# First and last transform stage on four 64x64 quarters of the PE array, third stage in two halves through one PSUM bank

## The chip, the core and the metric

The kernel runs on one core of a Trainium2 chip. A core has a matrix engine (TensorE; PE in the profile, its weight loads PEld), VectorE (DVE), ScalarE (ACT), GpSimd (POOL) and SyncE (SP), whose queue issues all DMAs of this kernel. Data lies in SBUF and PSUM, both with 128 partitions; matmuls write PSUM, which has 8 banks of 2 KB per partition. A matmul holds one operand as weights in the array and streams the other through it. The metric is the device time of one execution in microseconds (us).

## The reference

A Fourier layer on 8 sequences of 3136 x 256 float32 values, then a gated feed-forward layer with a convolution of three taps:

```python
X = np.fft.rfft(x, axis=1)
Yr = Xr @ w_r - Xi @ w_i + b_r
Yi = Xr @ w_i + Xi @ w_r + b_i
Yr = np.sign(Yr) * np.maximum(np.abs(Yr) - lam, 0.0)      # and Yi
y = np.fft.irfft(Yr + 1j * Yi, n=3136, axis=1)
h = np.maximum(y @ w_in, 0.0)                             # 256 -> 1024
conv_out[t] = sum(conv_w[k] * h[t + k - 1] for k in range(3))
out = (h * sigmoid(conv_out)) @ w_out                     # 1024 -> 256
```

## The kernel before

The transform of 3136 = 49 x 64 points is done by tables, in four stages.

Stage 1 takes transforms of 49 points. A row n of x is read as (n, j) with 98 values of n and 32 of j; x rows of even and odd n belong to two different transforms, so that a table `f1` of 98 x 98 holds two 49-point transforms beside each other, with zeros between. The work of one sequence (batch, 8 of them) is cut into 8 chunks of 4 values of j. A chunk is loaded by `load_x` into `xr` (98 partitions x 4 x 256), `stage1` makes two float32 matmuls of 512 columns, ScalarE copies each into `a1`, and one DMA stores `a1` in DRAM (`sc1`). `stage1_head` does the 8 chunks of the first batch at the start, all at once.

Stage 2 (`load_a2`, `stage2`) takes 64-point transforms of groups of 4 frequencies; `mix` multiplies by the complex weights in split precision (36 matmuls, `ps_mx`, L329), `threshold` cuts, and `stage3` transforms back by 64 points (12 matmuls, L361, into a PSUM tile of two banks, one copy of 1024 columns, one store to `sc2`). 50 groups (items) go through this as a software pipeline: iteration `it` does stage 2 of item `it`, the mix of item `it - 1`, the threshold of `it - 2` and stage 3 of `it - 3`. The order of PE, DVE and ACT is the order in which the code is written here. Stage 1 of the later batches is put between, as pieces that `one(k)` gives out at four places of an iteration; the numbers `due` say how many pieces are to be done by when (13 pieces in five iterations in the steady part, two pieces to a chunk).

In the second part, `stage4` takes the last transform, back by 49 points. It loads `z2` from `sc2` (100 partitions, 4 values of j, 256 values); z2 is the weights and the table `i2` (100 x 98, two 49-point transforms with zeros between) is streamed, in 8 matmuls per call; ScalarE and VectorE split the result into `yh` and `yl`. Then `up` and `down` do the feed-forward layer in chunks of 448 rows: 12 matmuls of 450 columns (L528), VectorE and ScalarE work for taps and gate, 21 matmuls of 256 columns (L556). The 8 calls of `stage4` per batch are put between these, for the batch after the one that the feed-forward layer is in; a scheduler at build time sets the final order of this part. All work of the first part must be done before its memory is free for the second.

float32 matmuls (stages 1, 2 and 4) show in the trace as two records each; those of type F32R show as one.

Of the kernel before, what the change touches and what calls it, by code (L numbers as in the profile page):

```python
# [9 lines left out]
F32 = mybir.dt.float32  # L10
# [9 lines left out]
R = 49  # L20
R2 = 64
# [14 lines left out]
def _tables():  # L36
    n = np.arange(R)
    n2 = np.arange(R2)
    u = np.arange(U + 1)

    f = np.zeros((R, 2, U + 1))
    ang = 2 * np.pi * ((n[:, None] * u[None, :]) % R) / R
    f[:, 0, :] = np.cos(ang)
    f[:, 1, :] = -np.sin(ang)
    fwd1 = np.zeros((R, 2, 2 * R))
    for h in range(2):
        for uu in range(1, U + 1):
            for c in range(2):
                fwd1[:, h, (uu - 1) * 4 + c * 2 + h] = f[:, c, uu]
# [6 lines left out]
    inv2 = np.zeros((2, 2 * (U + 1), R, 2))  # L56
    for i in range(2):
        inv2[i, :, :, i] = g.reshape(2 * (U + 1), R)
# [34 lines left out]
    return {  # L93
        "fwd1": fwd1.reshape(2 * R, 2 * R).astype(np.float32),
        "fwd2": fwd2.reshape(2 * R2, (U + 1) * 2 * SP).astype(np.float32),
        "inv1": inv1.reshape(2 * SP, U + 2, 2, 2, H).transpose(0, 1, 4, 3, 2).reshape(2 * SP, (U + 2) * 2 * R2).astype(np.float32),
        "inv2": inv2.reshape(4 * (U + 1), 2 * R).astype(np.float32),
    }


# [1 line left out]
def spectral_ffn_kernel(ctx: ExitStack, tc: tile.TileContext, x, w_r, w_i, b_r, b_i,  # L102
                        w_in, conv_w, w_out, fwd1, fwd2, inv1, inv2, out):
    nc = tc.nc
    K1, K2, KQ, KI = 2 * R, 2 * SP, 2 * R2, 4 * (U + 1)
# [16 lines left out]
    with ExitStack() as ab:  # L122
# [12 lines left out]
        f1 = c1.tile([K1, P], F32, name="f1")[:, 0:K1]  # L135
        t2 = c1.tile([KQ, U + 1, K2], F32, name="t2")
        cmx.tile([P, 96], F32, name="pad")
        bias = cmx.tile([P, 2, D], F32, name="bias")
# [101 lines left out]
                    yield None  # L240
                yield from work

        def load_x(pool, b, jc, parts=1, **kw):

            xr = pool.tile([K1, JC, D], F32, name="xr", **kw)
            xv = x[b].rearrange("(n j) d -> n j d", j=H)[:, jc * JC:(jc + 1) * JC, :]
            w = JC // parts
            for k in range(0, JC, w):
                ld = nc.sync.dma_start(xr[:, k:k + w, :], xv[:, k:k + w, :])
            return xr, ld  # L250

        def stage1(b, jc, xr):

            a1 = s1p.tile([K1, JC, D], F32, name="a1", bufs=3)
            for j in range(0, JC, 2):
                ps = ps1.tile([K1, 2, D], F32, name="ps_s1")
                nc.tensor.matmul(ps, f1, xr[:, j:j + 2, :], start=True, stop=True)  # L257
                nc.scalar.copy(a1[:, j:j + 2, :], ps)
                if j + 2 == JC:
                    nc.sync.dma_start(sc1[b][:, jc * JC:(jc + 1) * JC, :], a1)  # L260
                yield None

        def stage1_head(xs, b=0):

            with tc.tile_pool(name="ha", bufs=1, reuse_waits="tile") as ha:
                for jc, xr in enumerate(xs):
                    a1 = ha.tile([K1, JC, D], F32, name=f"ha{jc}")
                    for j in range(0, JC, 2):
                        k = (jc * 2 + j // 2) % 4
                        if k < 3:  # L270
                            ps = psm.tile([K1, 2, D], F32, name="ps_s1h", tag=f"ps_mx{k}")
                        else:
                            ps = ps1.tile([K1, 2, D], F32, name="ps_s1")
                        nc.tensor.matmul(ps, f1, xr[:, j:j + 2, :], start=True, stop=True)
                        if j:
                            nc.vector.tensor_copy(a1[:, j:j + 2, :], ps)
                        else:
                            nc.scalar.copy(a1[:, j:j + 2, :], ps)
                    st = nc.sync.dma_start(sc1[b][:, jc * JC:(jc + 1) * JC, :], a1)
            return st  # L280

        def load_a2(b, g):
# [71 lines left out]
        def stage3(b, g, s):  # L354

            sh, sl = s
            ps = psa.tile([KQ, UG, D], F32, name="ps_s3")
            for k in range(UG):
                u = g * UG + k if g < NG else U + k % 2
                for n, (lt, rh) in enumerate(((i1_hi, sh), (i1_hi, sl), (i1_lo, sh))):  # L360
                    nc.tensor.matmul(ps[:, k, :], lt[:, u, :], rh[:, k, :], start=(n == 0), stop=(n == 2))  # L361
            z1 = io.tile([KQ, UG, D], F32, name="z1", bufs=2)
            nc.scalar.copy(z1, ps)
            if g < NG:
                nc.sync.dma_start(sc2[b][:, g * UG:(g + 1) * UG, :], z1)
            else:
                for k in range(UG):
                    nc.sync.dma_start(sc2[b + k][:, U, :], z1[:, k, :])

        def some(g, n):  # L370
            for _ in range(n):
# [56 lines left out]
        for it in range(n_it + 3):  # L428
            xs[it], vs[it - 1] = [], []
            two = stage2(items[it][1], a2s.pop(it), xs[it]) if it < n_it else iter(())  # L430
            mx = mix(xs.pop(it - 1), vs[it - 1]) if 0 <= it - 1 < n_it else iter(())
            due = (2, 5, 9, 13, 16)[it] if it < 5 else 16 + 3 * (it - 4) if it <= 10 else 34 + 13 * (it - 10) // 5
            n_a, given = due - given, due
            work = 5 <= it < n_it

            def one(k=0):
# [17 lines left out]
            some(mx, 8)  # L454
            back(1)
            ss[it - 2] = next(th, None)
            one(1)
            some(two, 1)
            some(mx, 5)
            if it - 1 in i1s:  # L460
# [2 lines left out]
            some(th, 1)  # L463
            some(two, 1)
            back(1)
            some(mx, 5 if n_a > 3 else 9)
            one(2)
            some(th, 1)
            some(mx, 9)
            one(3)  # L470
            some(mx, 64)
            if held:
                held[:] = [0] * (next(background, None) == "act")
            if 0 <= it - 3 < n_it:
                stage3(*items[it - 3], ss.pop(it - 3))
            one(0)
            if it + 2 < n_it:
                a2s[it + 2], ld = load_a2(*items[it + 2])

# [8 lines left out]
    wk.tile([P, 24], F32, name="pad", bufs=1)  # L488
    psh, pso = pool("psh", 2, space=PSUM), pool("pso", space=PSUM)

    JG = 4
    NPC = H // JG

    def new_y(b):
        y = [(y_a, y_b)[b % 2].tile([P, NT, SW], F32R, name=nm) for nm in ("yh", "yl")]
# [3 lines left out]
            nc.vector.memset(qf[:, :, S + 1:S + 2], 0.0)  # L499
        return y  # L500

    def stage4(b, jg, y):

        z2 = zio.tile([KI, JG, D], F32, name="z2")
        nc.sync.dma_start(z2, sc2[b].rearrange("(j q) u e -> (q u) j e", q=4)[:, jg * JG:(jg + 1) * JG, :])
        ps = psh.tile([P, NT, 512], F32, name="ps_s4", tag="ps_h")
        for t in range(NT):
            for j in range(JG):
                nc.tensor.matmul(ps[:, t, j * K1:(j + 1) * K1], z2[:, j, t * P:(t + 1) * P], i2, start=(j == 0), stop=(j == JG - 1),  # L509
                                 skip_group_check=True)  # L510
        src = ps[:, :, 0:JG * K1].rearrange("p t (j m) -> p t m j", j=JG)

        def view(q):
            return q[:, :, 1:S + 1].rearrange("p t (m j) -> p t m j", j=H)[:, :, :, jg * JG:(jg + 1) * JG]
        nc.scalar.copy(view(y[0]), src)
        nc.vector.tensor_tensor(view(y[1]), src, view(y[0].bitcast(F32)), op=ALU.subtract)  # L516

# [109 lines left out]
```

## Time and profile before

| | us |
|---|---|
| median of 3 runs | 1760.06 (1758.44 to 1760.09) |
| the profiled execution, its own time | 1759.99 |
| span of its trace | 1758.2 |
| chain of work that ended last: share of stage 1 (L257) | 5% |
| the same: stage 4 (L509) | 6% |
| the same: feed-forward (L528, L556) | 31% and 31% |
| the same: mix (L329), stage 2 (L301), stage 3 (L361) | 11%, 5%, 3% |

The span runs from the first to the last instruction; the rest of the time lies around it. A row of a group gives line, engine, operation, tiles, shapes and count, then the busy time in us and the mean time of one in ns, then the idle time of the engine before them and what ended it. Records of matmuls overlap, since one is issued while the one before it still runs: the spacing of starts is what a matmul costs in a dense row, not its length. A row of the timeline or of the chain gives start, length, engine, line and how many like it stand together.

### The profile page before, as it was taken

The numbers are of one execution on the slowest core, as the hardware profiler recorded it, in microseconds if no ns is written. First come the engines' busy times: TensorE is split into PE (matmuls) and PEld (weight loads), VectorE is DVE, ScalarE is ACT, GpSimd is POOL, SyncE is SP. The second block draws the span as 40 slices with busy tenths as digits, with TensorE's granted clock in tenths as the row PEclk, the third lists the DMA queues.
The fourth block names the chain that finished last, engine by engine and source line by source line (L and its number), as shares of the span: only waits on it lengthen the run. The fifth ranks groups of instructions, "written<-read, shape, count | busy, mean of one in ns | idle before, by whom it ended". The sixth has DMA issues, their size and how long they took to land.

```text
span 1758.2 us, 28865 instructions
## 1 busy us (share of the span) xinstructions
PE 1721.6 (98%) x11872; PEld 1602.2 (91%) x11872; DVE 1472.0 (84%) x1757; ACT 1206.8 (69%) x1565; POOL 118.7 (7%) x54
## 2 busy tenths in 40 slices
PE   5999999999999999999999999999999999999999
PEld 2788888888988999999999999999999999999998
DVE  2778988889995988888888888888888888888887
ACT  2567677677665777677777777777777777777766
POOL 0122222222230000000000000000000000000000
PEclk8999999999998999999999999999999999999999
DMA  7877777767434110111111011111101111100001
GB/s 223 256 233 240 226 230 237 232 204 234 141 104 126 42 48 22 41 50 50 41 50 50 22 40 50 50 40 50 50 22 41 50 50 41 50 22 22 22 22 43
DMA packets 108305, 165.48 MB, mean 94 GB/s; under 512 B 8492, under 2 KB 86316, under 8 KB 108174
## 3 DMA queue, kind: packets, MB, share of 16 engines
q1 hardware_dynamic: 108174, 163.64, 29.4%
q8 instruction: 94, 1.54, 0.4%
q14 instruction: 37, 0.30, 0.1%
HBM read 86.02 MB, written 77.59 MB: 93 GB/s over the span
## 4 chain that ended last, share of the span: by engine, by line
PE 93%; DMA 2%; DVE 2%; issue 1%; ACT 0%; SPq 0%; DVEq 0%; ACTq 0%
PE ps_h L528 31%; PE acc L556 31%; PE ps_mx L329 11%; PE ps_s L509 6%; PE ps_s L257 5%; PE ps_s L301 5%; PE ps_s L361 3%; DMA t<-in_fwd_dram 1%; DMA z<-sc 1%; DVE v L337 0%; DMA sc<-a 0%; DVE p L333 0%; DMA sc<-ha 0%; DVE fl L307 0%; DVE v L348 0%
## 5 line engine op out<-in xcount | busy, mean ns | idle before, releaser
L556 PE MATMUL acc<-wout,gh 128*128 128x256 f32 x3136 | 567.4, 280 | 0.0
L528 PE MATMUL ps_h<-yh,win 128*128 128x450 f32 x1792 | 550.6, 368 | 0.0
L537 DVE SCALAR_TENSOR_TENSOR c<-h,cw,c 128x896 f32<-128x896 f32 x448 | 512.9, 1147 | 38.9 <-ACT c L535 37.3
L556 PEld LDWEIGHTS acc<-wout,gh 128*128 128x128 f32 x3136 | 490.1, 188 | 5.1
L556 PE MATMUL acc<-wout,gl 128*128 128x256 f32 x1568 | 437.4, 280 | 0.0
L530 ACT ACTIVATE h<-ps_h 128x900 f32<-128x900 f32 x224 | 207.4, 926 | 261.1 <-PE ps_h L528 261.1
L528 PEld LDWEIGHTS ps_h<-yh,win 128*128 128x128 f32 x1792 | 339.4, 189 | 26.1 <-DVE yl L516 0.4
L528 PE MATMUL ps_h<-yl,win 128*128 128x450 f32 x896 | 329.7, 368 | 0.0
L543 DVE TENSOR_TENSOR gl<-c,gh 128x896 fp32r<-128x896 f32 x224 | 243.0, 1088 | 76.3 <-ACT gh L542 74.7
L556 PEld LDWEIGHTS acc<-wout,gl 128*128 128x128 f32 x1568 | 293.8, 188 | 0.6
L539 DVE TENSOR_TENSOR c<-h,c 128x896 f32<-128x896 f32 x224 | 243.1, 1086 | 48.2 <-ACT c L538 48.2
L542 ACT CAST gh<-c 128x896 fp32r<-128x896 f32 x224 | 211.0, 942 | 70.2 <-DVE c L539 68.3
L538 ACT ACTIVATE c<-c 128x896 f32<-128x896 f32 x224 | 213.0, 951 | 8.2 <-DVE c L537 4.4
L329 PE MATMUL ps_mx<-wmix_hi,fl 128*128 128x256 f32 x600 | 185.2, 309 | 2.8 <-DVE fl L311 2.8
L329 PE MATMUL ps_mx<-wmix_hi,fh 128*128 128x256 f32 x600 | 183.7, 306 | 0.7 <-DVE v L337 0.6
L528 PEld LDWEIGHTS ps_h<-yl,win 128*128 128x128 f32 x896 | 169.4, 189 | 11.0
L535 ACT ACTIVATE c<-h,cw 128x896 f32<-128x896 f32 x168 | 176.1, 1048 | 2.2 <-DVE gl L543 0.2
L329 PE MATMUL ps_mx<-wmix_lo,fh 128*128 128x256 f32 x600 | 168.6, 281 | 0.0
L351 POOL TENSOR_TENSOR sl<-v,sh 128x1024 fp32r<-128x1024 f32 x50 | 118.5, 2370 | 410.7 <-PE ps_s L361 254.1
L337 DVE TENSOR_TENSOR v<-ps_mx,p 64x512 f32<-64x512 f32 x200 | 137.4, 687 | 2.9
L301 PEld LDWEIGHTS ps_s<-t,a 128*128 128x128 f32 (+1 forms) x800 | 99.7, 198 | 39.6 <-issue 28.8
L509 PEld LDWEIGHTS ps_s<-i,z 100*128 100x128 f32 x1024 | 128.1, 198 | 5.8 <-issue 3.0
(84 smaller groups left out, 1959.2 us busy)
## 6 DMA issues: line engine op xcount, KB each, us to landing
z<-sc SPq DMA_DIRECT2D x64, 400.0 KB
xr<-in_x_dram SPq DMA_DIRECT2D x63, 392.0 KB
a<-sc SPq DMA_DIRECT2D x48, 512.0 KB
sc<-z SPq DMA_DIRECT2D x48, 512.0 KB
out_dram<-o SPq DMA_DIRECT2D x27, 896.0 KB
sc<-a SPq DMA_DIRECT2D x56, 392.0 KB
sc<-ha SPq DMA_DIRECT2D x8, 392.0 KB
win_bits<-in_moe_w_in_dram SPq DMA_DIRECT2D x4, 512.0 KB
```

The costliest lines, as they stand in the source:

```text
L301: nc.tensor.matmul(ps[:, k], a2[0:rows, k, t * P:(t + 1) * P], t2[0:rows, u, :], start=(k == 0), stop=(k == UG - 1), skip_group_check=True)
L329: nc.tensor.matmul(ps[c][:, k, :], lt, rh, start=(n == 0), stop=(n == len(mm) - 1))
L509: nc.tensor.matmul(ps[:, t, j * K1:(j + 1) * K1], z2[:, j, t * P:(t + 1) * P], i2, start=(j == 0), stop=(j == JG - 1), skip_group_check=True)
L528: nc.tensor.matmul(ps[:, a, 0:CH + 2], lt, rh, start=(n == 0), stop=(n == len(mm) - 1))
L530: nc.scalar.activation(h, ps[:, :, 0:CH + 2], AF.Relu)
L535: nc.scalar.mul(c, h[:, :, 0:CH], cw[:, 0, f:f + 1])
L537: nc.vector.scalar_tensor_tensor(c, h[:, :, k:k + CH], cw[:, k, f:f + 1], c, op0=ALU.mult, op1=ALU.add)
L538: nc.scalar.activation(c, c, AF.Sigmoid)
L539: nc.vector.tensor_tensor(c, h[:, :, 1:CH + 1], c, op=ALU.mult)
L542: nc.scalar.copy(gh, c)
L543: nc.vector.tensor_tensor(gl, c, gh.bitcast(F32), op=ALU.subtract)
L556: nc.tensor.matmul(acc[m // 2][:, m % 2, :], lt[:, sl], rh[:, f, :], start=(f == 0 and n == 0 and m % 2 == 0), stop=(f == NF - 1 and n == ...
```

## The change

Stage 1 and stage 4 each use the array as four quarters of 64 rows x 64 columns. The tables lose their zeros: `f1` becomes 49 x 49 (in 64 columns), stored twice, at partitions 0 and 64; `i2` becomes 50 x 49, stored twice in the same way.

In stage 1 a chunk keeps its size. `load_x` now brings even and odd n to partitions 0 to 48 and 64 to 112, in two DMAs. `quarters` makes four matmuls of 512 columns: row half h (even or odd n), column half c (which two of the four j). The results of one h lie in one PSUM bank, and there are two such banks. `a1` is stored in two DMAs, one for each c, in pieces of 2 KB instead of 4 KB. A chunk is one piece of the schedule instead of two, so `due` is halved, and there are two places in an iteration for it.

In stage 4 a call takes 8 values of j and 128 of the 256 values instead of 4 and 256: 32 matmuls with 50 rows of weights, 64 columns of weights and 49 streamed columns, over row halves o and column halves c. Its two loads bring pieces of 512 bytes instead of 1 KB. The number of calls is the same.

Stage 3 goes in two halves of 6 matmuls through one PSUM bank, which pays for the second bank of stage 1; the second half stands at the end of the iteration, after the rest of the mix.

```diff
-        fwd1[:, h, 4 * U + h] = f[:, 0, 0]
+    fwd1 = np.zeros((2, SP, SP))
+    for uu in range(1, U + 1):
+        for c in range(2):
+            fwd1[:, :R, (uu - 1) * 2 + c] = f[:, c, uu]
+    fwd1[:, :R, 2 * U] = f[:, 0, 0]
...
-        ps1 = ab.enter_context(tc.tile_pool(name="ps1", bufs=1, space=PSUM))
+        ps1 = ab.enter_context(tc.tile_pool(name="ps1", bufs=2, space=PSUM))
...
+            xr = pool.tile([P, JC, D], F32, name="xr", **kw)
+            xv = x[b].rearrange("(n h j) d -> h n j d", h=2, j=H)
+            for h in range(2):
+                ld = nc.sync.dma_start(xr[h * SP:h * SP + R], xv[h, :, jc * JC:(jc + 1) * JC, :])
...
+        def quarters(ps, xr):
+
+            for c in range(2):
+                for h in range(2):
+                    rows = slice(h * SP, h * SP + R)
+                    nc.tensor.matmul(ps[h][c * SP:(c + 1) * SP], f1[rows, :], xr[rows, 2 * c:2 * c + 2, :], start=True, stop=True)
+
+        def store_a1(b, jc, a1):
+
+            for c in range(2):
+                j = jc * JC + 2 * c
+                st = nc.sync.dma_start(sc1[b].rearrange("(w h) j d -> w h j d", h=2)[:, :, j:j + 2, :], a1[c * SP:c * SP + R])
+            return st
...
-            ps = psa.tile([KQ, UG, D], F32, name="ps_s3")
+            for h in range(0, UG, 2):
+                ps = psa.tile([KQ, 2, D], F32, name="ps_s3")
...
+                nc.scalar.copy(z1[:, h:h + 2, :], ps)
+                if h == 0:
+                    yield None
...
+            due = (due + 1) // 2
...
-    JG = 4
-    NPC = H // JG
+    JG = 8
+    NPC = H // JG * NT
...
+        js, t = slice(n // NT * JG, (n // NT + 1) * JG), n % NT
+        z2 = zio.tile([P, JG, P], F32, name="z2")
+        z2v = sc2[b].rearrange("(j o c) u e -> o (c u) j e", o=2, c=2)
+        for o in range(2):
+            nc.sync.dma_start(z2[o * R2:o * R2 + KI], z2v[o, :, js, t * P:(t + 1) * P])
+        ps = psh.tile([P, 2, 512], F32, name="ps_s4", tag="ps_h")
+        for j in range(JG):
+            for o in range(2):
+                rows = slice(o * R2, o * R2 + KI)
+                for c in range(2):
+                    half = slice(c * R2, (c + 1) * R2)
+                    nc.tensor.matmul(ps[half, o, j * R:(j + 1) * R], z2[rows, j, half], i2[rows, :], start=(j == 0), stop=(j == JG - 1),
+                                     skip_group_check=True)
```

What this does to the order. First TensorE in a steady iteration, around a piece of stage 1 within the mix. Before (L329 is the mix into `ps_mx`, L257 a matmul of stage 1):

```order
L329 MATMUL ps_mx_322<-wmix_hi,fh 128x256
L329 MATMUL ps_mx_322<-wmix_lo,fh 128x256
L257 MATMUL ps_s_334<-xr,f_113 98x512
L329 MATMUL ps_mx_322<-wmix_hi,fl 128x256
L329 MATMUL ps_mx_322<-wmix_hi,fh 128x256
```

Now (L335 is the mix, L254 a matmul of stage 1 in one quarter), at the same place:

```order
L335 MATMUL ps_mx_704<-wmix_lo,fh 128x256
L254 MATMUL ps_s_723<-xr,f_113 64x512
L254 MATMUL ps_s_724<-xr,f_113 64x512
L254 MATMUL ps_s_723<-xr,f_113 64x512
L254 MATMUL ps_s_724<-xr,f_113 64x512
L335 MATMUL ps_mx_704<-wmix_hi,fl 128x256
L335 MATMUL ps_mx_704<-wmix_hi,fh 128x256
```

The four quarters of a chunk stand together, the two row halves taking turns; 56 such groups of four lie between matmuls that use the whole array.

Second, TensorE in the feed-forward part, where a call of stage 4 stands between `up` and `down`. Before (L528 is `up`, L509 stage 4, L556 `down`):

```order
L528 MATMUL ps_h<-yl,win_78 128x450
L528 MATMUL ps_h<-yh,win_79 128x450
L509 MATMUL ps_s_7529<-i_76,z_7527 128x98 x8
L556 MATMUL acc_7287<-wout_80,gh 128x256
L556 MATMUL acc_7287<-wout_81,gh 128x256
```

Now (L543 is `up`, L524 stage 4, L571 `down`):

```order
L543 MATMUL ps_h<-yl,win_78 128x450
L543 MATMUL ps_h<-yh,win_79 128x450
L524 MATMUL ps_s_8285<-i_76,z_8282 64x49 x32
L571 MATMUL acc_8042<-wout_80,gh 128x256
L571 MATMUL acc_8042<-wout_81,gh 128x256
```

The place is the same; eight matmuls have become 32 smaller ones.

Third, the queue of SP in the steady transform. Before (L249 loads x, L260 stores stage 1's result, L365 stage 3's, L286 loads for stage 2):

```order
L249 DMA xr<-in_x_dram 98x1024
L260 DMA sc_5_62<-a_2879 98x1024
L180 DMA wout_bits<-in_moe_w_out_dram 128x2x512
L249 DMA xr<-in_x_dram 98x1024
L365 DMA sc_3_68<-z_2988 128x1024
```

Now (L246 loads x, L260 stores, L374 stage 3's store, L292 loads for stage 2):

```order
L246 DMA xr<-in_x_dram 49x1024 x2
L260 DMA sc_5_62<-a_3141 98x1x512 x2
L178 DMA wout_bits<-in_moe_w_out_dram 128x2x512
L374 DMA sc_3_68<-z_3171 128x1024
L292 DMA a_3455<-sc_4_61 128x4x256
```

Each load and each store of a chunk is now two DMAs, over 49 partitions of SBUF each (the store's rows are written as the 98 rows of DRAM that it fills).

More of the change, by code (lines that the diff above doesn't have):

```diff
@@ L55, in _tables @@
     g = np.roll(g, -1, axis=1)
-    inv2 = np.zeros((2, 2 * (U + 1), R, 2))
-    for i in range(2):
-        inv2[i, :, :, i] = g.reshape(2 * (U + 1), R)
+    inv2 = np.zeros((2, R2, R))
+    inv2[:, 0:2 * (U + 1)] = g.reshape(2 * (U + 1), R)
     fwd2 = np.zeros((2, R2, U + 1, 2, SP))
@@ L241, in later, with load_x @@
                 yield from work
[L243 to L249, printed above, removed]
-            return xr, ld
-        def stage1(b, jc, xr):
[L254 to L261, printed above, removed]
+        def load_x(pool, b, jc, **kw):
+            xr = pool.tile([P, JC, D], F32, name="xr", **kw)
+            xv = x[b].rearrange("(n h j) d -> h n j d", h=2, j=H)
+            for h in range(2):
+                ld = nc.sync.dma_start(xr[h * SP:h * SP + R], xv[h, :, jc * JC:(jc + 1) * JC, :])
+            return xr, ld
+        def quarters(ps, xr):
[8 more added lines that the diff above has]
+            return st
+        def stage1(b, jc, xr):
+            a1 = s1p.tile([P, 2, JC // 2, D], F32, name="a1", bufs=3)
+            ps = [ps1.tile([P, JC // 2, D], F32, name="ps_s1") for h in range(2)]
+            quarters(ps, xr)
+            for h in range(2):
+                nc.scalar.copy(a1[:, h], ps[h])
+            store_a1(b, jc, a1)
+            yield None
         def stage1_head(xs, b=0):
@@ L266, in stage1_head @@
                 for jc, xr in enumerate(xs):
[L267 to L279, printed above, removed]
+                    a1 = ha.tile([P, 2, JC // 2, D], F32, name=f"ha{jc}")
+                    if jc % 2:
+                        ps = [psm.tile([P, JC // 2, D], F32, name="ps_s1h", tag=f"ps_mx{h}") for h in range(2)]
+                    else:
+                        ps = [ps1.tile([P, JC // 2, D], F32, name="ps_s1") for h in range(2)]
+                    quarters(ps, xr)
+                    nc.scalar.copy(a1[:, 0], ps[0])
+                    nc.vector.tensor_copy(a1[:, 1], ps[1])
+                    st = store_a1(b, jc, a1)
             return st
@@ L356, in stage3 @@
             sh, sl = s
-            ps = psa.tile([KQ, UG, D], F32, name="ps_s3")
[L358 to L361, printed above, removed]
-            z1 = io.tile([KQ, UG, D], F32, name="z1", bufs=2)
-            nc.scalar.copy(z1, ps)
+            z1 = io.tile([KQ, UG, D], F32, name="z1", bufs=2)
+            for h in range(0, UG, 2):
+                ps = psa.tile([KQ, 2, D], F32, name="ps_s3")
+                for k in range(h, h + 2):
+                    u = g * UG + k if g < NG else U + k % 2
+                    for n, (lt, rh) in enumerate(((i1_hi, sh), (i1_hi, sl), (i1_lo, sh))):
+                        nc.tensor.matmul(ps[:, k - h, :], lt[:, u, :], rh[:, k, :], start=(n == 0), stop=(n == 2))
+                nc.scalar.copy(z1[:, h:h + 2, :], ps)
+                if h == 0:
+                    yield None
             if g < NG:
@@ L368, in stage3 @@
                     nc.sync.dma_start(sc2[b + k][:, U, :], z1[:, k, :])
+            yield None
         def some(g, n):
@@ L456, in spectral_ffn_kernel @@
             ss[it - 2] = next(th, None)
-            one(1)
+            one(0)
             some(two, 1)
@@ L465, in spectral_ffn_kernel @@
             back(1)
-            some(mx, 5 if n_a > 3 else 9)
-            one(2)
+            some(mx, 9)
+            some(s3, 1)
             some(th, 1)
-            some(mx, 9)
-            one(3)
             some(mx, 64)
@@ L473, in spectral_ffn_kernel @@
                 held[:] = [0] * (next(background, None) == "act")
-            if 0 <= it - 3 < n_it:
-                stage3(*items[it - 3], ss.pop(it - 3))
-            one(0)
+            some(s3, 1)
+            one(1)
             if it + 2 < n_it:
@@ L500, in new_y, with stage4 @@
         return y
[L502 to L511, printed above, removed]
+    def stage4(b, n, y):
+        js, t = slice(n // NT * JG, (n // NT + 1) * JG), n % NT
[11 more added lines that the diff above has]
+                                     skip_group_check=True)
+        src = ps[:, :, 0:JG * R].rearrange("p o (j m) -> p o m j", j=JG)
         def view(q):
-            return q[:, :, 1:S + 1].rearrange("p t (m j) -> p t m j", j=H)[:, :, :, jg * JG:(jg + 1) * JG]
+            return q[:, t, 1:S + 1].rearrange("p (m o j) -> p o m j", o=2, j=H)[:, :, :, js]
         nc.scalar.copy(view(y[0]), src)
```

18 lines of the change are left out of this document (7 added, 11 removed).

## The prediction

> **What bounds the kernel now.** I read the page first: busy time of each engine, then the chain of work that ended last.
>
> ```profile
> PE 1721.6 (98%) x11872; PEld 1602.2 (91%) x11872; DVE 1472.0 (84%) x1757; ACT 1206.8 (69%) x1565; POOL 118.7 (7%) x54
> PE 93%; DMA 2%; DVE 2%; issue 1%; ACT 0%; SPq 0%; DVEq 0%; ACTq 0%
> ```
>
> TensorE is busy 98% of the span and is 93% of the chain, so what it gains or loses is gained or lost by the kernel, unless another engine is close behind. That differs by stage, so next comes the table by stretches (busy of PE, PEld, DVE, ACT, POOL, granted clock, DMA share, GB/s):
>
> ```profile
> 0.00:32.00 32.00, 19.70 (x32) 6.30 (x32) 8.53 (x15) 7.53 (x13) 0.20 (x4) 0.96 0.76 227
> 32.00:96.00 64.00, 54.55 (x341) 44.59 (x342) 40.65 (x68) 35.88 (x63) 7.08 (x3) 0.89 0.79 237
> 96.00:443.00 347.00, 344.93 (x2453) 296.57 (x2452) 300.72 (x499) 244.67 (x397) 84.96 (x36) 1.00 0.72 229
> 525.00:562.00 37.00, 33.38 (x208) 32.02 (x208) 14.57 (x20) 17.07 (x18) 2.37 (x1) 0.82 0.48 141
> 562.00:1745.00 1183.00, 1183.00 (x8135) 1139.28 (x8134) 1021.21 (x1021) 846.29 (x995) 0.00 (x0) 1.00 0.13 40
> ```
>
> The opening and the first iterations wait for DMA. From 96 to 443 us (transform, with stage 1 of later batches between) PE is full, DMA at 0.72. From 562 (feed-forward, with stage 4 between) PE is full, DVE has 162 us to spare, and DMA is nearly idle.
>
> **The change, part by part.** The prices of the two stages now, from groups and the chain:
>
> ```profile
> L257 PE MATMUL ps_s<-xr,f 98*98 98x512 f32 x224 | 114.9, 593 | 0.8 <-ACT a L258 0.7
> L509 PE MATMUL ps_s<-i,z 100*128 100x98 f32 x1024 | 128.0, 281 | 3.6 <-DMA z<-sc 2.6 <-DVE yl L516 1.1
> 51.38 0.86 PE ps_s L257 x2
> 533.94 1.78 PE ps_s L509 x16
> ```
>
> Each float32 matmul leaves two records, two passes one behind the other (112 matmuls of L257, x224). A stage-1 pass of 512 columns is 0.43 us and a chunk of two matmuls 1.72. A stage-4 call of 8 matmuls is 16 passes at 0.111, 1.78 us. A 98-column pass streams in 0.43 x 98/512 = 0.082, so 0.111 is the load of 128 weight columns, not the streaming.
>
> *Passes.* Afterwards a chunk is 4 matmuls of 512 columns, 8 passes, twice as many; a stage-4 call is 32 matmuls, 64 passes of 49 columns with 64 weight columns each, four times as many. An estimate by columns from the rows above: 0.056 for the load, 0.041 for the streaming. So all hangs on how many quarters work at once. The nearest rows:
>
> ```profile
> 202.53 1.02 PE L257 MATMUL ps_s<-xr,f 98*98 98x512 f32 x2
> 202.99 0.68 PE L329 MATMUL ps_mx<-wmix_hi,fl 128*128 128x256 f32 x1
> 203.51 0.28 PE L329 MATMUL ps_mx<-wmix_hi,fh 128*128 128x256 f32 x1
> ```
>
> The matmul issued at 202.99 takes 0.68 instead of 0.28, standing behind the second pass: matmuls keep their written order. The two passes of a matmul use the same quarter, so the second waits for the first, and the next quarter's first pass stands behind that second one. At best the second pass of one runs beside the first of the next: 8 stage-1 passes take 5 x 0.43 = 2.15, not 2 x 0.43. One after another they take 3.44; all four side by side 0.86. I take 2.15. In stage 4, 64 weight loads one after another are 3.58; loads overlapped but passes in order, 33 x 0.056 = 1.85; all side by side 0.90; and if a pair of load and matmul is never faster than the 0.111 of L509, 7.1. I take 3.58: the load is the bound in L509, and no row shows two loads at once.
>
> The Trainium skill, page TensorEngine Tiling (Array Packing), section Key Properties, says that different tiles of the array can load weights and multiply in parallel, which speaks for this change; by it the chunk would be 0.86 and the call 0.90. No run here shows it; the case is a rival below.
>
> *Changes of shape.* One iteration of before uses 64 rows of the array instead of 128:
>
> ```profile
> 455.91 0.28 PE L361 MATMUL ps_s<-sl,i_hi 128*128 128x256 f32 x1
> 456.03 0.27 PE L361 MATMUL ps_s<-sh,i_lo 128*128 128x256 f32 x1
> 456.23 2.05 PE L301 MATMUL ps_s<-t,a 64*128 64x128 f32 x16
> 458.21 0.38 PE L329 MATMUL ps_mx<-wmix_hi,fh 128*128 128x256 f32 x1
> 458.44 0.28 PE L329 MATMUL ps_mx<-wmix_lo,fh 128*128 128x256 f32 x1
> 199.80 1.95 PE L301 MATMUL ps_s<-t,a 128*128 128x128 f32 x16
> 201.71 0.28 PE L329 MATMUL ps_mx<-wmix_lo,fh 128*128 128x256 f32 x1
> 456.23 1.86 PEld L301 LDWEIGHTS ps_s<-t,a 64*128 64x128 f32 x16
> ```
>
> From the last L361 to the second ps_mx it takes 458.44 - 456.03 = 2.41. At full shape the same is 201.71 - 199.80 = 1.91 plus one spacing of 0.12, so 2.03: 0.38 us for going in and out. The first weight load starts only at 456.23, with the first matmul, so nothing of it is hidden. Going in costs half a weight load less with 64 columns, so 0.35 for each group of quarters.
>
> So a chunk goes from 1.72 to 2.15 + 0.35 = 2.50, **+0.78**; a stage-4 call from 1.78 to 3.58 + 0.35 = 3.93, **+2.15**.
>
> *DMA.* The x loads and the stage-1 stores become pairs over 49 partitions. How many of the 16 engines a DMA uses can be counted by its closing marks, the packets under 512 B:
>
> ```profile
> DMA packets 7814, 8.04 MB, mean 40 GB/s; under 512 B 160, under 2 KB 7799, under 8 KB 7799
> out_dram<-o SPq DMA_DIRECT2D x5, 896.0 KB
> z<-sc SPq DMA_DIRECT2D x8, 400.0 KB
> DMA packets 108305, 165.48 MB, mean 94 GB/s; under 512 B 8492, under 2 KB 86316, under 8 KB 108174
> xr<-in_x_dram SPq DMA_DIRECT2D x63, 392.0 KB
> cw_bits<-in_moe_conv_w_dram SPq DMA_DIRECT2D x3, 8.0 KB
> ```
>
> In 600 to 800 us 5 stores over 128 partitions and 8 loads over 100 leave 160 marks: 5 x 16 + 8 x 10. Over the whole span 8492 less 3072 packets of 8 bytes (cw_bits, 3 x 8 KB) and 198 rows of 392 bytes (f, i) is 5222, which 172 DMAs at 16, 65 of 100 partitions at 10 and 130 of 98 at 14 give exactly. So the count is the largest number up to 16 that divides the partitions; for 49 it is 7, for the z loads of 50 still 10. The Trainium skill's page DMA: Bandwidth & Descriptors, section Why a DMA increments its semaphore by 16 and not by 1, states this rule and that the lowest-numbered engines are taken; the marks agree with the counts, and which engines they are no row shows.
>
> If the seven are always the same, they carry all of x and of the stores. A busy engine moves 229 / (16 x 0.72) = 19.9 GB/s. A chunk is 0.80 MB: 5.8 us on seven engines, 2.9 on fourteen. An iteration's a2 and z1 are 1.05 MB on sixteen: 3.3 us. With 1.3 chunks (6.5 in five iterations, by `due`) it is 1.3 x 5.8 + 3.3 = 10.8 us per iteration on those seven. Before:
>
> ```profile
> 203.55 3.27 PE ps_mx L329 x28
> 252.18 3.27 PE ps_mx L329 x28
> 18.00:23.00 5.00, 4.36 (x11) 1.48 (x10) 2.74 (x5) 2.11 (x4) 0.00 (x0) 1.00 0.90 345
> ```
>
> five iterations in 48.63, 9.73 each. PE will need 9.73 + 1.3 x 0.78 = 10.74. The two are level: I take 10.85, **+40 us** over the 347/9.73 = 35.7 iterations. The last row is a fast stretch, 345/(16 x 0.90) = 24 GB/s; at that DMA needs 8.9, and PE alone gives +36.
>
> *Opening.* Stage 2 starts when batch 0's stores have landed:
>
> ```profile
> 26.63 4.83 DMA sc<-ha
> 31.73 0.38 SPq L286
> 88.82 7.12 DMA sc<-a
> 95.95 3.90 DMA a<-sc
> ```
>
> x and stores of one batch are 6.42 MB: 23 us on fourteen engines, 46 on seven, 38 at 24 GB/s. **+19** (15 to 23). From 32 to 96 us, ended by waits for batch 1's stores, half of the 15.2 MB is of this kind: 51 us of work at fourteen engines, 79 at seven (65 at the fast rate), in 64. **+15** (0 to 28).
>
> *Stage 4 and the rest.*
>
> ```profile
> 525.65 4.71 DMA z<-sc
> 535.73 6.04 DMA z<-sc
> L258 ACT COPY a<-ps_s 98x512 f32<-98x512 f32 x112 | 66.1, 590 | 36.8 <-PE ps_s L257 36.7
> L363 ACT COPY z<-ps_s 128x1024 f32<-128x1024 f32 x50 | 50.6, 1011 | 24.5 <-PE ps_s L361 22.9 <-DMA xr<-in_x_dram 1.0
> ```
>
> 54 calls lie in full PE time: 54 x 2.15 = 116. The other ten stand at 525 to 562, where the two waits (10.7 us) hide half of 21.5: 11. **+127.** At nothing: stage 3 in halves. Its second half waits for the copy of the first (512 columns, 0.59 like L258's), and about 15 matmuls of the mix at 0.12 (1.8 us) stand between; without that cover it is 0.6 x 50 = 30 us. Two copies of 0.59 for one of 1.01 add 8.5 us to ACT, which idles 30% there. SP issues four DMAs a chunk for two; its issues take 0.4 us (31.73), so 1.3 x 2 x 0.4 = 1 us of a 9.73 iteration, and only the x loads and a2 loads queue behind them, asked for an iteration or more ahead. Stage 4's 512-byte pieces, twice the packets, hide behind a DMA share of 0.13.
>
> Sum: 19 + 15 + 40 + 127 = +201, on the profiled execution's 1759.99 (the median is 1760.06): **1961**.
>
> **The rivals.**
> *Loads overlap too:* 1.85 + 0.35 in stage 4, +0.42 a call, 54 calls and some, +23: 1760 + 19 + 15 + 40 + 23 = 1857. For it: at 456 loads of a 64-row tile already run under the matmuls of the same tile. Against: these are one load at a time.
> *No overlap at all* (the change doesn't do what it says): a chunk costs 3.44 + 0.35, +2.07; iterations of 12.4 us, +96 instead of 40: 2017. Nothing speaks against it in the trace.
> *A floor of the pair:* 7.1 + 0.35 a call, +5.67: 54 x 5.67 + 46 = 352 instead of 127: 2186. Against: 0.111 fits a weight load of 128 columns.
> *Faster: all quarters side by side.* Chunk 1.21, call 1.25 (-0.53): stage 4 gives 64 x 0.53 = -34. Stage 1 gives 9.07 an iteration on PE, but counts only if the seven DMA engines run at 24 GB/s (8.9): 35.7 x 0.66 = -24. With the opening at +15: 1717. It decides where second passes no longer hold back the next quarter; with the slow DMA rate it is 1800. Against it: the written order seen at 202.99.
>
> **How the numbers follow.** Forecast 40%; loads overlap 22%; no overlap 15%; floor 10%; faster 8%, its slow-DMA form 3%; 2% lands within 0.2% (about what a measurement can tell from no change). So faster 0.08, same 0.02, slower 0.90. The range leaves out the floor, the faster case and the 2%: from 1800 (slow-DMA form) to 2050 (no overlap with the opening at +51: 2034, and 16 for the two estimates by columns).
>
> **What would show it.** A stage-4 group x64 near 3.9 us and its spacing (0.056, 0.03 or 0.11); a stage-1 group x8 near 2.2; 0.35 us around each; marks of 7 per x load; the first a2 load at about 50 us; iterations of 10.8. I am wrong if passes of different quarters start at once across the second passes, or if the seven DMA engines change from DMA to DMA.

## The result and the profile after

The changed kernel takes **1776.25 us** (median of 4 runs, 1775.88 to 1778.64) against 1759.53 for the kernel before, beside it on the same chip: ratio 1.0099, 95% interval 1.0081 to 1.0116. It is slower, by 17 us; 201 were forecast, and the range began at 1800.

The page of the changed kernel, rows of busy time, closing marks and chain:

```profile
PE 1679.1 (95%) x15200; PEld 1538.5 (87%) x15200; DVE 1470.9 (83%) x1757; ACT 1205.5 (68%) x1615; POOL 119.0 (7%) x54
DMA packets 140799, 165.90 MB, mean 93 GB/s; under 512 B 9184, under 2 KB 112608, under 8 KB 140640
PE 79%; DMA 16%; DVE 2%; ACT 1%; issue 1%; SPq 1%; POOL 0%; ACTq 0%; DVEq 0%; POOLq 0%
```

TensorE has 42 us less to do although it has 3328 more records, and DMA has gone from 2% of the chain to 16%. The kernel did not become slower on the array; it became slower in front of it. The groups of the two stages and the same table by stretches as before (busy PE, PEld, DVE, ACT, POOL, granted clock, DMA share, GB/s):

```profile
L524 PE MATMUL ps_s<-i,z 50*64 50x49 f32 x4096 | 79.3, 226 | 7.5 <-DMA z<-sc 5.3 <-DVE yl L531 2.3
L254 PE MATMUL ps_s<-xr,f 49*64 49x512 f32 x480 | 79.0, 661 | 17.0 <-DVE ha L284 10.5 <-DMA xr<-in_x_dram 6.5
```

```profile
0.00:32.00 32.00, 15.13 (x56) 4.28 (x60) 6.76 (x13) 6.67 (x12) 0.20 (x4) 1.00 0.48 167
32.00:96.00 64.00, 37.60 (x258) 27.85 (x251) 26.77 (x44) 22.89 (x43) 2.65 (x2) 0.79 0.64 194
96.00:443.00 347.00, 320.23 (x2527) 273.18 (x2526) 287.55 (x480) 240.10 (x417) 80.34 (x34) 0.96 0.65 219
562.00:1745.00 1183.00, 1171.33 (x11089) 1106.49 (x11088) 1022.12 (x1028) 844.01 (x1003) 4.71 (x2) 0.99 0.15 43
```

Four times the passes of stage 4 take 79 us instead of 128. From 96 to 443 us TensorE, full before, now stands idle for 27 us, at a DMA share that *fell* from 0.72 to 0.65. In the first 32 us the share is 0.48 instead of 0.76: transfers are waited for while half of the DMA engines rest.

Where the spans part, by four places read from the timeline (the first stage 2, its 11th and 46th, the first `up` of the feed-forward part, the end; the forecast's stretches end at 32, 96, 443 and 562 us, so its terms match the rows only roughly):

| us | before | after | difference | term of the forecast |
|---|---|---|---|---|
| to the first stage 2 | 35.9 | 49.8 | +13.9 | +19 |
| ten iterations | 105.7 | 110.5 | +4.8 | +15 |
| the next 35 | 331.1 | 349.1 | +18.0 | +40 |
| to the first `up` | 79.4 | 84.2 | +4.8 | +11 |
| feed-forward with stage 4 | 1206.1 | 1180.8 | -25.3 | +116 |
| sum | 1758.2 | 1774.4 | +16.2 | +201 |

### The profile page after: what moved, and what is told of

Same layout as the page of the kernel before. It is cut to its first block, busy times and chain, and to the rows that moved or that the text cites. A ratio compares the mean times of both kernels' runs of the same rounds, so it can differ in the third digit from the quotient of the medians.

```text
span 1774.4 us, 35604 instructions
## 1 busy us (share of the span) xinstructions
PE 1679.1 (95%) x15200; PEld 1538.5 (87%) x15200; DVE 1470.9 (83%) x1757; ACT 1205.5 (68%) x1615; POOL 119.0 (7%) x54
## 2 busy tenths in 40 slices
DMA packets 140799, 165.90 MB, mean 93 GB/s; under 512 B 9184, under 2 KB 112608, under 8 KB 140640
## 4 chain that ended last, share of the span: by engine, by line
PE 79%; DMA 16%; DVE 2%; ACT 1%; issue 1%; SPq 1%; POOL 0%; ACTq 0%; DVEq 0%; POOLq 0%
PE acc L571 32%; PE ps_h L543 31%; PE ps_mx L335 5%; DMA sc<-z 4%; PE ps_s L524 4%; DMA sc<-a 4%; DMA xr<-in_x_dram 4%; PE ps_s L307 3%; PE ps_s L369 2%; DMA a<-sc 2%; PE ps_s L254 2%; DMA t<-in_fwd_dram 1%; DMA z<-sc 1%; DMA wm_raw<-in_w_i_dram 1%; DVE v L343 0%
## 5 line engine op out<-in xcount | busy, mean ns | idle before, releaser
L571 PE MATMUL acc<-wout,gh 128*128 128x256 f32 x3136 | 567.7, 281 | 1.5 <-ACT gh L557 1.5
L543 PE MATMUL ps_h<-yh,win 128*128 128x450 f32 x1792 | 550.4, 368 | 5.3 <-DVE yl L531 5.3
L571 PEld LDWEIGHTS acc<-wout,gh 128*128 128x128 f32 x3136 | 491.2, 188 | 10.4 <-ACT gh L557 1.9
L571 PE MATMUL acc<-wout,gl 128*128 128x256 f32 x1568 | 436.9, 280 | 0.0
L543 PEld LDWEIGHTS ps_h<-yh,win 128*128 128x128 f32 x1792 | 339.1, 189 | 31.5 <-DVE yl L531 5.6
L543 PE MATMUL ps_h<-yl,win 128*128 128x450 f32 x896 | 329.7, 368 | 0.0
L571 PEld LDWEIGHTS acc<-wout,gl 128*128 128x128 f32 x1568 | 293.6, 188 | 0.1
L543 PEld LDWEIGHTS ps_h<-yl,win 128*128 128x128 f32 x896 | 169.5, 189 | 11.2
L335 PE MATMUL ps_mx<-wmix_hi,fh 128*128 128x256 f32 x600 | 172.9, 288 | 0.5 <-DVE v L343 0.5
L335 PE MATMUL ps_mx<-wmix_hi,fl 128*128 128x256 f32 x600 | 172.2, 287 | 0.6 <-DVE fl L317 0.6
L335 PE MATMUL ps_mx<-wmix_lo,fh 128*128 128x256 f32 x600 | 168.0, 280 | 0.0
L307 PEld LDWEIGHTS ps_s<-t,a 128*128 128x128 f32 (+1 forms) x800 | 105.4, 212 | 51.5 <-issue 27.6
L307 PE MATMUL ps_s<-t,a 128*128 128x128 f32 (+1 forms) x800 | 111.6, 299 | 35.6 <-DMA a<-sc 25.8
L335 PEld LDWEIGHTS ps_mx<-wmix_hi,fl 128*128 128x128 f32 x600 | 113.1, 189 | 33.7 <-issue 32.5
```

The costliest lines, as they stand in the source:

```text
L307: nc.tensor.matmul(ps[:, k], a2[0:rows, k, t * P:(t + 1) * P], t2[0:rows, u, :], start=(k == 0), stop=(k == UG - 1), skip_group_check=True)
L335: nc.tensor.matmul(ps[c][:, k, :], lt, rh, start=(n == 0), stop=(n == len(mm) - 1))
L543: nc.tensor.matmul(ps[:, a, 0:CH + 2], lt, rh, start=(n == 0), stop=(n == len(mm) - 1))
L571: nc.tensor.matmul(acc[m // 2][:, m % 2, :], lt[:, sl], rh[:, f, :], start=(f == 0 and n == 0 and m % 2 == 0), stop=(f == NF - 1 and n == ...
```

## Do the quarters work side by side?

The timeline of the changed kernel around one chunk of stage 1 (start, length, engine, line):

```profile
306.52 0.28 PE L335 MATMUL ps_mx<-wmix_hi,fh 128*128 128x256 f32 x1
306.64 0.28 PE L335 MATMUL ps_mx<-wmix_lo,fh 128*128 128x256 f32 x1
306.85 1.09 PE L254 MATMUL ps_s<-xr,f 49*64 49x512 f32 x8
307.87 0.38 PE L335 MATMUL ps_mx<-wmix_hi,fl 128*128 128x256 f32 x1
308.09 0.28 PE L335 MATMUL ps_mx<-wmix_hi,fh 128*128 128x256 f32 x1
```

Measured as in the forecast, to the second full-array matmul behind the chunk and less two spacings of 0.12, the chunk costs 308.09 - 306.64 - 0.24 = 1.21 us, both changes of shape in it. The forecast took 2.50 for this, and its faster rival 1.21. The eight records of the chunk one by one (starts of the matmuls, and of the weight loads ahead of them; each of the four matmuls in the code has two):

```
weight loads, first passes    306.844  306.851  306.857  306.864
matmuls,      first passes    306.846  306.852  306.859  306.866
weight loads, second passes   306.899  306.906  306.912  306.919
matmuls,      second passes   307.326  307.332  307.339  307.346
next full-array matmul        307.865
```

The first passes of all four quarters start 6 to 7 ns apart, and 0.48 us later the four second passes. Though the code writes four whole matmuls one behind another, a second pass waits only for its own quarter, and the next quarter's first pass does not stand behind it. Four loads, too, run at once. One call of stage 4 in the same view:

```profile
599.75 0.36 PE L543 MATMUL ps_h<-yh,win 128*128 128x450 f32 x1
600.04 1.15 PE L524 MATMUL ps_s<-i,z 50*64 50x49 f32 x64
601.12 0.47 PE L543 MATMUL ps_h<-yh,win 128*128 128x450 f32 x1
601.43 0.37 PE L543 MATMUL ps_h<-yl,win 128*128 128x450 f32 x1
601.64 0.37 PE L543 MATMUL ps_h<-yh,win 128*128 128x450 f32 x1
```

Two matmuls of `up` in a row start 0.21 apart (601.64 - 601.43), so the call costs 601.43 - 599.75 - 0.42 = 1.26 us with its changes of shape.

The 64 passes start in groups of four, 6 to 7 ns apart within a group (600.134, .140, .147, .154) and 0.058 us from group to group (.192, .250, .309): 16 x 0.058 = 0.93. So the estimate of 0.056 for a pass of 64 weight columns was good; it was to be counted 16 times and not 64.

**Quarter after quarter.** If this depends on consecutive matmuls lying in different quarters, another order of the same 32 matmuls must lose it. The changed kernel with

```diff
-        for j in range(JG):
-            for o in range(2):
-                for c in range(2):
+        for o in range(2):
+            for c in range(2):
+                for j in range(JG):
```

> The changed kernel with the 32 matmuls of a stage-4 call written quarter after quarter (eight of one quarter, then the next) instead of taking turns. If matmuls of different quarters keep the written order, the passes of a quarter run one after another: 64 x 0.056 + 0.35 = 3.9 us a call instead of 1.25, 1776 + 54 x 2.7 = about 1920. If each quarter takes its matmuls when it is free, whatever stands before them for other quarters: 1776 (1772 to 1785).

Measured: 1951.62 us, ratio 1.1109 [1.1093, 1.1126]. Its timeline, and the stretch of 800 to 900 us in it and in the changed kernel:

```profile
710.63 3.35 PE L524 MATMUL ps_s<-i,z 50*64 50x49 f32 x64
```

```profile
800.00:900.00 100.00, 100.00 (x897) 95.03 (x896) 76.03 (x75) 62.80 (x75) 0.00 (x0) 0.97 0.15 43
```

```profile
800.00:900.00 100.00, 100.00 (x1001) 94.26 (x1001) 87.37 (x91) 71.22 (x84) 0.00 (x0) 1.00 0.16 44
```

A call takes 3.35 us instead of 1.15, 2.2 x 64 = 141 us more. Within a quarter the passes start 0.058 apart, one at a time; only at the border of two quarters do some overlap, which is why it is 3.35 and not 64 x 0.058 = 3.71. The other 34 of the 175 us are about what the granted clock (the figure ahead of the DMA share) would cost, 0.97 instead of 1.00: 3% of some 1200 us is 36. That the clock is lower with this order is seen, not explained. So matmuls do keep their written order where a quarter is busy, as the forecast said, and its 3.93 for a call is near the price of *this* order; what it missed is that the code takes turns.

**Each stage alone.** The kernel before with the stage 4 of the changed kernel (its loads, tables and 32 matmuls a call), and the changed kernel with the stage 4 of before:

> The kernel before with only the fourth stage (and its table) of the changed kernel. A call at 1.25 us instead of 1.78 gives 64 x 0.53 = 34 us by all theories: 1726 (1720 to 1735). If the halved packets of its loads cost something at the change of parts, up to 10 us of that is missing.

> The changed kernel with the fourth stage (and its table) of the kernel before. If the two parts add, 1776 + 34 = 1810 (1800 to 1815) by all theories: the whole loss lies in the transform part.

Measured: stage 4 alone 1738.12 us, 0.9881 [0.9866, 0.9896]; stage 1 and the third stage in halves alone 1794.73, 1.0204 [1.0188, 1.0219]. The two add up: -21 and +36 are +15, against +17. Stage 4 alone stays short of the 34 us that were expected of it. It brings 25.3 us in the feed-forward part in both kernels that have it (1180.8 there), and 5 to 6 are given back between the 46th stage 2 and the first `up`; whether its 512-byte loads do that wasn't tried. The loss is wholly on the side of stage 1.

## What costs 17 us, and 36 without the new stage 4?

The closing marks say how many engines each DMA used. Of 9184, the small table loads are 3072 + 256; 128 loads and 128 stores of 49 partitions at 7, 128 z loads at 10, 172 DMAs at 16 and two at 16 are 5856, and the sum is exactly 9184. In the opening the table by stretches of 2 us shows the seven at work. Here are two rows of before, the first with x loads alone, the second with loads of the mix weights beside them:

```profile
2.00:4.00 2.00, 0.00 (x0) 0.00 (x0) 0.00 (x0) 0.22 (x2) 0.00 (x0) 1.00 0.86 237
12.00:14.00 2.00, 2.00 (x3) 0.66 (x3) 0.69 (x1) 0.00 (x0) 0.00 (x0) 1.00 0.98 236
```

And here is the changed kernel, where up to then only x loads run:

```profile
12.00:14.00 2.00, 2.00 (x10) 0.44 (x7) 0.00 (x0) 0.22 (x1) 0.00 (x0) 1.00 0.44 180
```

Before, 0.86 is near 14/16. Now 7/16 is 0.44: seven engines full, nine at rest, though the loads of several chunks have been issued. Sixteen such loads queue on the same seven. The Trainium skill, page DMA: Bandwidth & Descriptors, section Why a DMA increments its semaphore by 16 and not by 1, says that a DMA from this kind of queue takes the lowest-numbered engines, so each time the same ones; the 0.44 agrees, which the forecast could only suppose. A busy engine moves 180/7 = 25.7 GB/s here, but this is no fixed rate: in the second row of before it is 236/(16 x 0.98) = 15.1. The transform then waits; the chain of the changed kernel has pieces of this kind:

```profile
211.66 10.34 DMA sc<-z
222.72 0.97 PE ps_s L369 x6
223.69 1.16 PE ps_s L254 x8
260.59 11.78 DMA a<-sc
272.45 9.84 DMA sc<-a
```

`sc<-z` (the store of stage 3) and `a<-sc` (the load for stage 2) use all sixteen engines; by this account they end only when their share on the seven has gone through, which no row shows by itself.

**All transfers wide.** The changed kernel with loads and stage-1 stores cut into 48 partitions (16 engines) and one:

```diff
+            js = slice(jc * JC, (jc + 1) * JC)
             for h in range(2):
-                ld = nc.sync.dma_start(xr[h * SP:h * SP + R], xv[h, :, jc * JC:(jc + 1) * JC, :])
+                nc.sync.dma_start(xr[h * SP + R - 1:h * SP + R], xv[h, R - 1:R, js, :])
+            for h in range(2):
+                ld = nc.sync.dma_start(xr[h * SP:h * SP + R - 1], xv[h, 0:R - 1, js, :])
...
-                st = nc.sync.dma_start(sc1[b].rearrange("(w h) j d -> w h j d", h=2)[:, :, j:j + 2, :], a1[c * SP:c * SP + R])
+                to = sc1[b].rearrange("(w h) j d -> w h j d", h=2)[:, :, j:j + 2, :]
+                nc.sync.dma_start(to[R - 1:R], a1[c * SP + R - 1:c * SP + R])
+                st = nc.sync.dma_start(to[0:R - 1], a1[c * SP:c * SP + R - 1])
```

> The changed kernel with each x load and each stage-1 store cut at 48 + 1 partitions, so that the large piece can use 16 DMA engines instead of 7; packets, tables, matmuls and order as in the changed kernel. Theory 1 (seven engines hold the transform): the opening is back at about 32 us before the first load for stage 2, steady iterations fall to the 9.07 us of TensorE, so 1760 - 24 (stage 1) - 34 (stage 4) = about 1700 (1690 to 1720). Theory 2 (more and smaller packets and DMAs): these stay, with two more DMAs per pair, so 1776 or more. Theory 3 (the new places of stage 1 and stage 3 in halves): 1776.

**Narrow without the quarters.** The kernel before, with its 98 partitions cut into 49 and 49 in the same transfers:

> The kernel before with each x load and each stage-1 store cut at 49 + 49 partitions, 4 KB packets as before, nothing else. Theory 1: both pieces run on seven engines, +19 and +15 in the opening and 10.8 instead of 9.73 us per iteration: 1810 to 1835. Theory 2 (packet size): packets are the same, only the number of DMAs doubles: 1760 to 1765. Theory 3: 1760.

Measured: 1733.35 us, 0.9858 [0.9842, 0.9875] for the wide one: 43 us gained by nothing but the shape of transfers, and the changed kernel would beat the one before, though by less than expected: its opening did not come back (more on this below). 1783.87, 1.0135 [1.0118, 1.0152] for the narrow one: +25 without any quarter, less than the 50 and more that its theory 1 had. But 21 of the 25 lie in the opening and the first ten iterations; its steady iterations take 9.67 us as before, while the changed kernel needs 10.25 (stage 2 of the 11th item to that of the 31st, by 20).

**A buffer?** Among the waits of the changed kernel (us in all, times, longest) is ScalarE's for the store of stage 3, of which two buffers exist:

```profile
ACT z L370 <- DMA sc<-z: 40.2, 11, 6.6
```

The changed kernel with `z1` cut into two half tiles of 3 and 2 buffers, stored apart:

> The changed kernel with stage 3's result tile cut in two, three buffers for the first half and two for the second, each half stored by a DMA of its own. In the changed kernel ScalarE waited 40 us in all for an earlier store of this tile before it could copy the first half. Theory 1a (that buffer wait is what makes the iterations 10.2 us): most of it goes, 1740 to 1755. Theory 1b (the seven engines are simply full): the time only moves to other waits for DMA, 1770 to 1780.

Measured: 1774.71, 1.0100 [1.0080, 1.0119]. No gain beyond the noise: this wait falls from 40.2 to 18.0 us, but ScalarE's wait for the store of stage 1 (`ACT a L269 <- DMA sc<-a`) grows from 7.4 to 24.8. The wait is where the lateness is seen, not where it comes from. This run keeps stage 3 in halves, so it says nothing of them; the runs with one half of the transfers wide, below, do.

**Fourteen engines.** 56 partitions per transfer instead of 49 (`sc1` with 112 rows): 14% more bytes, of which the seven extra rows a half are not used.

```diff
-                ld = nc.sync.dma_start(xr[h * SP:h * SP + R], xv[h, :, jc * JC:(jc + 1) * JC, :])
+                ld = nc.sync.dma_start(xr[h * SP:h * SP + n], xv[h, :, jc * JC:(jc + 1) * JC, :])
...
-                st = nc.sync.dma_start(sc1[b].rearrange("(w h) j d -> w h j d", h=2)[:, :, j:j + 2, :], a1[c * SP:c * SP + R])
+                st = nc.sync.dma_start(sc1[b].rearrange("(w h) j d -> w h j d", h=2)[:, :, j:j + 2, :], a1[c * SP:c * SP + RP])
```

(`n` is `RP` = 56, and 49 for the last sequence, behind which there are no rows to read.)

> The changed kernel with x loads and stage-1 stores over 56 partitions instead of 49 (seven more rows, which nothing uses; the last batch's loads stay at 49; sc1 is longer by 14 rows), so that 14 engines share them, at 14% more bytes and no more DMAs. Theory 1: seven engines were the loss; iterations at 9.1 us, opening within 5 us of the kernel before: 1720 (1710 to 1735). Theory 2 (packet size, number of DMAs): nothing gained, and 14% more bytes: 1776 to 1785.

Measured: 1715.21, 0.9765 [0.9750, 0.9780], some 60 us below the changed kernel. The closing marks show the fourteen: 10864, which is 9184 and seven more for each of 112 loads and 128 stores. The stretch of 96 to 443 us in it:

```profile
96.00:443.00 347.00, 346.77 (x2871) 301.29 (x2868) 327.62 (x547) 269.75 (x463) 90.33 (x38) 1.00 0.79 255
```

TensorE is full again, and an iteration takes 9.0 us. This also beats the wide form, which needs twice as many issues: the opening of that kernel on SP's queue shows them, 32 stores one behind another, of which the last three and what follows are

```profile
38.83 0.58 SPq L265 DMA_DIRECT2D sc<-ha  x1
39.44 0.59 SPq L264 DMA_DIRECT2D sc<-ha  x1
40.08 0.58 SPq L265 DMA_DIRECT2D sc<-ha  x1
43.30 0.38 SPq L297 DMA_DIRECT2D a<-sc  x1
```

At 0.6 us or more each, 32 are some 20 us, so its first `a<-sc` leaves at 43.30, hardly before the 45.82 of the changed kernel.

**The head first.** The same kernel, with the stage 1 of the first sequence written ahead of the loads of the mix weights, whose copies on VectorE and ScalarE stood before those of stage 1:

```diff
             with tc.issue_after(ld.ins):
+                st = stage1_head(xh)
+            with tc.issue_after(st.ins):
                 load_mix()
                 load_t2(0)
-                st = stage1_head(xh)
```

> The kernel of the 56 rows, with the first batch's stage 1 and its stores written ahead of the loads and splits of the mixing weights. In the changed kernel VectorE waited 13.4 us in the opening for a weight that was loaded behind the x loads, with the copies of stage 1 queued behind it. If that wait sets the opening: 5 to 10 us less than with the 56 rows alone. If the opening is set by DMA bandwidth alone: the same within 2 us.

Measured: 1709.90, 0.9730 [0.9714, 0.9746], the fastest of all that ran: some 65 us below the changed kernel, 2.7% below the one before. Its first `a<-sc`:

```profile
30.80 0.37 SPq L296 DMA_DIRECT2D a<-sc  x1
```

**Which transfers, and is it a limit or a stall?** Left was why 10.25, when the kernel of 49 and 49 partitions keeps 9.67 with the same bytes on seven engines. One suspect is the size of pieces (the quarters store 2 KB at a time, that kernel 4 KB), another the pace that TensorE asks for. Three kernels: that kernel with stores of 2 KB; the changed kernel with only its stores wide; and with only its loads wide.

> The kernel before with its loads and stores cut into 49 and 49 partitions took 1784 us and kept 9.7 us per steady iteration; the changed kernel, whose stores go in pieces of 2 KB, took 10.25. This one also cuts the stores into pieces of 2 KB, four DMAs a chunk. If the small pieces slow the seven engines (theory P): steady iterations of 10.2 us and 1795 to 1815 us in all. If the pieces don't matter and the changed kernel waits because its TensorE asks for a chunk every 9.1/1.3 us instead of every 9.7/1.3 (theory Q): iterations of 9.7 and 1780 to 1792.

> The changed kernel with only its stage-1 stores cut into 48 and 1 partitions; the loads stay at 49. Seven engines then carry about 1.2 MB per iteration instead of 1.5, 6.9 us at 25 GB/s each. If the seven engines are full by the sum of loads and stores (Q): iterations of 9.1 to 9.3 us, and 1740 to 1755 us in all. If the stores' pieces of 2 KB on seven engines are what slows (P): 1733 to 1742, as with both cut.

> The changed kernel with only its x loads cut into 48 and 1 partitions; the stores stay at 49, in pieces of 2 KB. By the sum on seven engines (Q): like the kernel with only the stores cut, 1740 to 1755 us. If the stores' pieces on seven engines are the cause (P): 1760 to 1776.

| | us | ratio, interval | steady iteration, us |
|---|---|---|---|
| 49 and 49, pieces of 2 KB | 1783.41 | 1.0149 [1.0129, 1.0169] | 9.67 |
| only stores wide | 1733.50 | 0.9863 [0.9849, 0.9878] | 9.0 |
| only loads wide | 1730.47 | 0.9843 [0.9827, 0.9860] | 9.0 |

The pieces don't matter. And either half of the cure is the whole (both together gave 1733.35 and 9.2 us). With only the stores wide the time is in the range of the theory of pieces, which the first row had already spoken against; with only the loads wide it is below what either theory had. One narrow stream through seven engines costs nothing in the steady part; the second tips it. The stretch from 96 to 443 us with only the loads wide:

```profile
96.00:443.00 347.00, 345.73 (x2866) 299.00 (x2863) 323.53 (x540) 271.67 (x468) 91.92 (x39) 1.00 0.75 245
```

The last kernel writes `quarters(ps, xr)` twice in `stage1`, the second time over the same result, so that TensorE has 49 us more to do:

> The changed kernel with the four matmuls of every chunk after the head written twice (the second time over the same result): 56 chunks cost 0.87 us more on TensorE, 1.1 us per steady iteration, 49 us in all. If the transfers on seven engines set the pace of the steady iterations (10.25 us where TensorE alone needs 9.05 and would now need 10.2), most of it is hidden: 1776 to 1790 us, iterations of 10.3 to 10.6. If each iteration instead adds a stall of its own to TensorE's work, whatever the pace: iterations of 11.3 and 1815 to 1830.

Measured: 1784.82, 1.0156 [1.0123, 1.0189], iterations of 10.14. Of 49 us, 40 vanish, and the stretch says where:

```profile
96.00:443.00 347.00, 343.74 (x2866) 275.91 (x2865) 284.55 (x473) 239.52 (x410) 78.42 (x34) 1.00 0.64 218
```

TensorE is now busy for 344 of 347 us, and its iterations are no longer than in the changed kernel: the added work fills the idle time of the waits. So the waits are no stall that comes on top of TensorE's work, however much that is.

The waits aren't the whole loss either. The granted clock of this stretch is 0.96 in the changed kernel and 1.00 here. In the changed kernel each of the six longest waits of TensorE in it (2.3 to 6.4 us) is followed by 3.4 or 6.8 us at half clock. The first of them:

```profile
115.20:118.60 3.40, 0.00 (x1) 0.00 (x0) 2.37 (x4) 1.80 (x5) 2.35 (x1) 1.00 0.11 37
118.70:125.40 6.70, 3.83 (x18) 3.86 (x19) 0.81 (x2) 0.90 (x3) 0.00 (x0) 0.50 0.94 322
```

The pieces at half clock add up to 30.7 us, which costs TensorE 15. With the 27 us that it stands idle this is 42 us in 33.9 iterations, 1.24 each: the difference between 10.25 and 9.0. The kernel with the doubled matmuls and that of 49 and 49 have one such piece in the stretch, of 3.4 us.

How full the seven engines are can be counted from the start and length of every packet in the trace. From the 11th to the 31st stage 2, seven packets or more are under way for 93% of the time in the changed kernel, for 95% in both kernels of 49 and 49, and for 91% in the last one. That puts the work of the seven per iteration at 9.5, 9.2, 9.2 and 9.3 us, as an estimate from above, since the records don't name the engine. TensorE, when it doesn't wait, needs 9.0, 9.67, 9.67 and some 10.1 (9.0 and 1.1 for the doubled matmuls). By this estimate the seven need longer than TensorE only in the changed kernel, and only there TensorE goes on waiting. With one stream wide the seven carry 1.2 MB of the 1.50 and have time to spare.

## Why the prediction was wrong, point by point

**Passes: the step that failed.** "The second waits for the first, and the next quarter's first pass stands behind that second one" was taken from the row at 202.99. The order seen there is true, but the matmul that waited needed the whole array, and the one before it used 98 rows and 98 columns: no part was free. It could say nothing of a matmul with a free quarter. Four quarters run their passes side by side (starts 7 ns apart), so a chunk is 1.21 us instead of 2.50.

**Weight loads: the same step again.** "No row shows two loads at once" was so because no tiles of before lie in different quarters. Four loads run at once, a call is 16 x 0.058, and the largest term of the sum, +127 for stage 4, has the wrong sign: -25.3 in the feed-forward part. The rival in which all quarters work side by side had 1.21 for the chunk, 1.25 for the call and -34 for stage 4. Measured are 1.21, 1.26 and, with stage 4 alone, -21. It had a chance of 8%, and of 3% with the slow DMA rate. The Trainium skill's page TensorEngine Tiling (Array Packing), section Key Properties, said that different tiles load and multiply in parallel; this case agrees, for matmuls of two passes too, as long as neighbours in the code lie in different quarters.

**Changes of shape.** 0.35 for a group holds: 1.21 less two passes (0.86) is 0.35.

**DMA: the right mechanism.** Seven engines per transfer, always the same seven, the first a2 load "at about 50" (45.82; 31.73 before): all as forecast; and since the kernel with nothing but its transfers made wide is faster than the one before, it is why this one became slower. The sizes were too large. An iteration's 1.50 MB on the seven (1.3 x 0.80, and 7/16 of 1.05) was put at 10.8 us, with 19.9 GB/s for each from a mean; by the count of packets it is 9.5 us, 22.6 GB/s. TensorE needs 9.0 beside it and not 10.74, so of the +1.1 us an iteration that the forecast had, 0.6 came (10.25 against 9.67). What the forecast had no term for is the clock: of the 1.24 us above 9.0, 0.8 are waits and 0.45 the half clock behind them. Why the waits come to 0.8, and not to the 0.5 that lie between 9.0 and 9.5, stays open.

**Opening.** +13.9 for +19, and +4.8 for +15: the right place, with the slow rate again. Part of the opening is order and not bandwidth: the copies of the weights stood ahead of those of stage 1, and moving them brought 5.3 us (1715.21 to 1709.90).

**At nothing.** Stage 3 in halves shows no price: with one half of the transfers wide, and its second half at the end of each iteration, TensorE is busy 345.73 of 347 us, and an iteration takes 9.0, against 9.07 in the forecast's sum without such a price. SP's extra issues show none in the changed kernel, but the still more numerous ones of the wide kernel do in its opening.

**Sum and range.** The last part of the table was too dear by 141 us, the four ahead of it, 85 for 41.5, by 43. The direction came out right because the DMA term is real, and in part by luck: the largest term had the wrong sign, and the smaller ones outweighed it. The case nearest to the result, all quarters side by side with the slow DMA rate, stood at 1800 with 3% and as the end of the range; its DMA terms (19 + 15 + 40) were twice what was measured in their places (36.7), which is why the time lies below the range.

## What to carry to other kernels

A transfer's partition count sets how many DMA engines carry it (by the closing marks 7 for 49, 14 for 56, 10 for 100, 16 for 128): count the marks, or look for a DMA share that stays at k/16 while something waits, and pad to a count with a large divisor up to 16 (56 for 49: 1715.21 us) rather than add a second transfer (1733.35). Matmuls in different quarters of the array run side by side, passes and weight loads, if the code takes turns between the quarters. A row that shows two instructions in order tells nothing of two that need different parts of the engine.

## What the hardware showed beside that

In the steady part narrow transfers cost nothing until the seven engines need longer than TensorE: with loads and stores narrow an iteration takes 10.25 us, with either of them wide 9.0, with both 9.2 (why not 9.0 wasn't tried). A TensorE that waits for transfers loses twice, 27 us idle and 15 at half clock in 347 us; given 49 us of useless work it ended 9 us later, and its granted clock in that stretch was 1.00 instead of 0.96. And 64 passes of stage 4 written quarter after quarter not only took 3.35 us instead of 1.15, but went with a granted clock of 0.97 instead of 1.00 over most of the second part.
